# Moving one filler block from in front of unit 5's A product to behind its y transposes, and unit 3's v cast one SiLU sooner

## Chip, cores and metric

One core of one Trainium2 chip. The time is device microseconds (us) of that core; lower is better. Each launch gives one time, and a profile can be taken with it.

## The reference

A linear-attention recurrence (batch 4, 8 heads, 768 tokens, head size 48) followed by a two-layer network with a SiLU (3072 tokens, width 384, hidden 2048):

```python
for t in range(S):
    cur = einsum('bhd,bhe->bhde', u * kt, vt)
    y[:, :, t] = einsum('bhd,bhde->bhe', rt, state + cur)
    state = w[None, :, :, None] * state + einsum('bhd,bhe->bhde', kt, vt)
x = y.transpose(0, 2, 1, 3).reshape(B * S, H * D)
h = x @ w_in                       # 384 -> 2048
out = (h / (1 + exp(-h))) @ w_out  # 2048 -> 384
```

## The kernel before

The sequence is cut into 6 chunks of 128 tokens; a "unit" is one chunk of one of the 4 batches, 24 in all. A unit's chain runs over several engines: transposes of r and k on TensorE (PE; `tr`, `tk` or `xs`), decays on VectorE (DVE; `rk`), the A product on PE (`ae`, `ao`), its mask on DVE (`am`), the y product on PE, the addition of the bonus `vu` on DVE (`y16`), transposes of y on PE (`yT`) and their copy on ScalarE (ACT; `xT`). GpSimd (POOL) makes the bonus (`ku`, `rku_f`, `vu`), scaled keys (`kc`) and decayed states (`sdec`).

So that PE has work while a unit's chain runs elsewhere, the network is cut into "fillers" in a list: a hidden block of the first layer (three matmuls here, weight 0.5, ended by a SiLU on ACT), or a quarter of an output of the second layer (four matmuls, weight 1). `fill(n)` takes blocks of weight n off the front of the list. The trace before shows PE and ACT taking their instructions in the order in which they are written: unit 3's y product waits until 25.48 us and the filler written behind it starts only then, at 25.68; and ACT casts unit 3's v at 24.93, without a pause behind the two SiLUs that began at 24.32, though POOL's `vu` had begun to read the same input at 23.75. (Weight loads, a row of their own called PEld, ran ahead there: the first for that product came at 24.99.)

```python
    def p2(i, spins=0, nxt=None, late=False):      # A product, then the masks
        ...
        for p in range(NP):
            nc.tensor.matmul(ae[:, p, :], L["kT"][0:D, p, :], L["rT"][0:D, p, :], ...)
            nc.tensor.matmul(ao[:, p, :], L["kT"][64:PR, p, :], L["rT"][64:PR, p, :], ...)
        if nxt is not None:
            p1t(nxt)                               # the next unit's transposes, xs
        for a in (ae, ao):
            nc.vector.tensor_tensor(out=am, in0=a, in1=maskM..., op=ALU.mult)

    def l1(sc, ft, b0=0, b1=B):                    # a hidden block
        hps = ps.tile([128, B * C], FP, name="hps", tag="moe", bufs=3)
        ...
        nc.scalar.activation(out=gts[sc][:, ft, b0 * C:b1 * C], in_=hps, func=AF.Silu)

    def fill(n):
        owed[0] = min(owed[0] + n, n + 1.0)
        while fillers and owed[0] > 0.01:
            w_, f = fillers.pop(0)
            owed[0] -= w_
            f()

    # unit 3                                  # unit 5 (b_)
    p2(3)                                     fill(.5)
    nc.scalar.copy(out=st[3], in_=zero)       p2(b_, nxt=b_ + 1, late=True)
    fill(1)                                   fill(1.5)
    nat_v(3)    # v cast on ACT               p3y(b_)     # y product
    fill(1)                                   p3e(b_)     # y16 on DVE
    p3y(3)                                    ...
    p3e(3)                                    fill(.5)
    ...                                       p4(b_)      # yT on PE, xT on ACT
                                              fill(1)
```

(The last block sets two places of the program side by side.)

## Time and profile before

| | before |
|---|---|
| median of 4 runs | 202.06 us (201.87 to 202.56) |
| span of the profiled run | 200.4 us |
| PE busy | 192.2 us, 96% |
| granted TensorE clock, profiled run | 0.997 of full |
| PE idle between 24 and 66 us | 1.66 us |
| PE idle between 66 and 194.7 us | none |

A row of the timeline below gives start, length, engine, line of the kernel, operation, tiles out and in, sizes and count; in brackets stands the idle time of the engine just before and what ended it. "hps" is a hidden block, "ops" an output quarter.

### The profile page before, as it was taken

What the parts mean: (1) busy time and instruction counts of PE and PEld (TensorE: products, weight loads), DVE (VectorE), ACT (ScalarE), POOL (GpSimd) and SP (SyncE); (2) the same over time, 40 slices, a digit from 0 to 9 for tenths busy, and PEclk for the clock granted to TensorE, in tenths of its full rate; (3) what the DMA queues carried; (4) which work ended last, traced back from release to release, by engine and by line L of the source; (5) the groups of instructions that cost most, each with busy time, mean ns of one, the idle gap of its engine ahead of it and who ended that gap; (6) DMA issues with size and microseconds to landing.
All of it is one profiled execution on the core that took longest, in us unless ns stands there. A gap on an engine that the chain in (4) does not pass through costs nothing.

```text
span 200.4 us, 5014 instructions
## 1 busy us (share of the span) xinstructions
PE 192.2 (96%) x1973; PEld 129.8 (65%) x1973; DVE 115.1 (57%) x233; ACT 98.1 (49%) x225; POOL 115.1 (57%) x145
## 2 busy tenths in 40 slices
PE   7889999899999999999999999999999999999993
PEld 2646878787766876765666764666764666644563
DVE  6787658885758539594646864646863635510121
ACT  2556587799132651139662039662039661069300
POOL 3499869989975674867593767481748370100000
PEclk9999999999999999999999999999999999999998
DMA  4999998999999922688721738201120001210022
GB/s 85 205 182 176 206 210 169 163 186 196 193 191 265 229 42 64 136 185 176 140 55 41 160 108 167 44 0 43 39 83 0 0 3 41 77 44 0 0 78 79
DMA packets 82207, 22.34 MB, mean 111 GB/s; under 512 B 75400, under 2 KB 82184, under 8 KB 82184
## 3 DMA queue, kind: packets, MB, share of 16 engines
q1 hardware_dynamic: 78504, 18.88, 43.7%
q0 software_dynamic: 3680, 3.15, 10.6%
q8 instruction: 15, 0.25, 0.5%
q14 instruction: 8, 0.07, 0.1%
HBM read 20.45 MB, written 4.72 MB: 126 GB/s over the span
## 4 chain that ended last, share of the span: by engine, by line
PE 86%; issue 4%; POOL 4%; DVE 3%; ACT 2%; POOLq 0%; DVEq 0%
PE ops L366 30%; PE hps L354 29%; PE ae L267 11%; PE xs L242 4%; PE y L293 3%; PE yT L342 2%; PE y L290 2%; PE sps L309 1%; PE ops L380 1%; DVE am L276 1%; POOL rku_f L186 1%; POOL ku L180 1%; DVE y L300 1%; ACT xT L343 1%; PE ao L269 1%
## 5 line engine op out<-in xcount | busy, mean ns | idle before, releaser
L357 ACT ACTIVATE gT<-hps 128x256 f16<-128x256 f32 (+1 forms) x128 | 59.6, 494 | 24.2 <-PE hps L354 22.4
L354 PE MATMUL hps<-xT,win 128*128 128x256 f16 (+1 forms) x384 | 69.9, 326 | 0.9 <-ACT xT L343 0.4
L366 PE MATMUL ops<-wout,gT 128*128 128x384 f16 x368 | 65.5, 326 | 0.0
L354 PEld LDWEIGHTS <-win 128*128 128x128 f16 x384 | 35.1, 98 | 22.7 <-issue 1.7
L366 PEld LDWEIGHTS <-gT 128*128 128x128 f16 x368 | 34.2, 98 | 21.1
L343 ACT COPY xT<-yT 128x384 f16<-128x384 f16 x24 | 11.4, 476 | 58.2 <-PE yT L342 58.1
L276 DVE TENSOR_TENSOR am<-ae,maskM 128x512 f16<-128x512 f32 x24 | 16.6, 692 | 36.6 <-PE ao L269 36.4
L203 POOL TENSOR_TENSOR vu<-vin,rku 128x384 f32<-128x384 f32 x23 | 19.1, 831 | 19.4 <-DVE rku L197 19.3
L370 DVE COPY osb<-ops 128x384 f32<-128x384 f32 x23 | 12.8, 556 | 29.2 <-PE ops L366 29.1
L267 PE MATMUL ae<-rk 48*128 48x128 f32 x192 | 27.7, 285 | 0.7 <-DVE rk L230 0.7
L267 PEld LDWEIGHTS ae<-rk 48*128 48x128 f32 x192 | 23.1, 187 | 7.9 <-issue 5.3
L269 PE MATMUL ao<-rk 48*128 48x128 f32 x192 | 27.7, 285 | 0.0
L253 DVE TENSOR_TENSOR rk<-xs,pif 112x512 f32<-112x512 f32 x40 | 25.6, 681 | 1.7 <-PE xs L242 1.7
L186 POOL TENSOR_TENSOR rku_f<-rin,ku 128x384 f32<-128x384 f32 x24 | 24.1, 1005 | 1.9
L180 POOL TENSOR_TENSOR ku<-kin,u_bc 128x384 f32<-128x384 f32 x24 | 24.1, 1005 | 1.6 <-DMA kin<-in_k_dram 1.5
L191 POOL TENSOR_TENSOR kc<-kin,lamC 128x384 f16<-128x384 f32 x24 | 24.1, 1005 | 0.0
L269 PEld LDWEIGHTS ao<-rk 48*128 48x128 f32 x192 | 23.1, 187 | 0.0
L323 POOL CAST stb<-st 112x384 f16<-112x384 f32 x12 | 6.0, 504 | 25.8 <-DVE st L318 25.8
L300 DVE TENSOR_TENSOR y<-y,vu 128x384 f16<-128x384 f32 x24 | 13.3, 554 | 8.6 <-PE y L293 7.2
L276 DVE TENSOR_TENSOR am<-ao,maskM 128x512 f16<-128x512 f32 x24 | 16.3, 681 | 0.0
L325 POOL TENSOR_TENSOR sdec<-st,pif 112x384 f32<-112x384 f32 x16 | 13.4, 838 | 2.2 <-ACT gT L357 1.1
L197 DVE TENSOR_REDUCE rku<-rku_f 128x8 f32<-128x384 f32 x24 | 13.2, 549 | 2.0 <-POOL rku_f L186 1.6
(74 smaller groups left out, 188.6 us busy)
## 6 DMA issues: line engine op xcount, KB each, us to landing
rin<-in_r_dram SPq DMA_DIRECT2D x24, 192.0 KB, 3.6
kin<-in_k_dram SPq DMA_DIRECT2D x24, 192.0 KB, 3.7
vin<-in_v_dram SPq DMA_DIRECT2D x24, 192.0 KB, 3.6
out_dram<-osb SPq DMA_DIRECT2D x23, 192.0 KB, 2.0
win<-in_moe_w_in_dram POOLq DMA_DIRECT2D x4, 384.0 KB, 5.8
wout<-in_moe_w_out_dram POOLq DMA_DIRECT2D x2, 768.0 KB, 10.5
out_dram<-osh SPq DMA_DIRECT2D x1, 128.0 KB, 1.7
out_dram<-osh SPq DMA_DIRECT2D x1, 64.0 KB, 1.5
```

Of the source, the lines that this page charges most:

```text
L180: nc.gpsimd.tensor_tensor(out=L["ku"], in0=kin[i % NIN][:, :, 0:D], in1=u_bc, op=ALU.mult)
L186: nc.gpsimd.tensor_tensor(out=L["rku_f"], in0=rin[i % NIN][:, :, 0:D], in1=L["ku"], op=ALU.mult)
L191: nc.gpsimd.tensor_tensor(out=kc[i % NKC][:, :, 0:D], in0=kin[n][:, :, 0:D], in1=lamC, op=ALU.mult)
L203: nc.gpsimd.tensor_tensor(out=L["vu"], in0=vin[i % NIN], in1=L["rku"].unsqueeze(2).broadcast_to([128, H, D]), op=ALU.mult)
L253: nc.vector.tensor_tensor(out=rk[:, :, :, 64 * g:64 * g + 64], in0=xs[g][0:PR], in1=lam(g), op=ALU.mult)
L267: nc.tensor.matmul(ae[:, p, :], L["kT"][0:D, p, :], L["rT"][0:D, p, :], start=True, stop=True)
L269: nc.tensor.matmul(ao[:, p, :], L["kT"][64:PR, p, :], L["rT"][64:PR, p, :], start=True, stop=True)
L276: nc.vector.tensor_tensor(out=am, in0=a, in1=maskM.unsqueeze(1).broadcast_to([128, NP, C]), op=ALU.mult)
L300: nc.vector.tensor_tensor(out=L["y16"], in0=L["y"], in1=L["vu"], op=ALU.add)
L354: nc.tensor.matmul(hps, win[:, q, ft * 128:(ft + 1) * 128], xts[sc][:, q, b0:b1, :].rearrange("p b t -> p (b t)"), start=(q == 0), stop=(q ...
L357: nc.scalar.activation(out=gts[sc][:, ft, b0 * C:b1 * C], in_=hps, func=AF.Silu)
L366: nc.tensor.matmul(ops, gts[sc][:, ft, b * C:(b + 1) * C], wout[:, ft, :], start=(ft == 0), stop=(ft == NFT - 1))
```

## The change

The aim is to take two waits from PE: the one of unit 3's y product for its v cast, and the one for the copy of unit 5's transposes, which blocks the first hidden block of the next chunk.

```diff
     p2(3)
+    fill(.5)
+    nat_v(3)
+    fill(1.5)
     nc.scalar.copy(out=st[3], in_=zero)
-    fill(1)
-    nat_v(3)
-    fill(1)
     p3y(3)
@@
         load(NIN + i)
-    fill(.5)
     p2(b_, nxt=b_ + 1, late=True)
     fill(1.5)
     p3y(b_)
```

Nothing is added to replace the `fill(.5)`: the list is simply one block behind from there on, so every later `fill` takes something else than before until the list runs empty near 87 us.

## The prediction

> **What bounds the kernel now.** I read the page first, its busy rows and its slices.
>
> ```profile
> span 200.4 us, 5014 instructions
> PE 192.2 (96%) x1973; PEld 129.8 (65%) x1973; DVE 115.1 (57%) x233; ACT 98.1 (49%) x225; POOL 115.1 (57%) x145
> ...
> PE   7889999899999999999999999999999999999993
> ...
> PEclk9999999999999999999999999999999999999998
> ```
>
> TensorE (PE) is busy for 96% of the span at full granted clock. The change adds and removes no instruction, so only PE's 8.2 us of idle time can change. A table of stretches (start:end, length, PE busy, ...) says where the idle time lies.
>
> ```profile
> 24.00:27.50 3.50, 3.22 (x37) 2.35 (x34) 1.72 (x3) 2.94 (x9) 1.89 (x3) 1.00 1.16 231
> 27.50:37.50 10.00, 9.91 (x152) 8.60 (x152) 8.21 (x17) 7.85 (x22) 9.05 (x11) 1.00 0.96 178
> 37.50:48.50 11.00, 10.10 (x134) 8.32 (x133) 8.17 (x18) 9.18 (x27) 9.76 (x12) 1.00 1.23 178
> 48.50:63.00 14.50, 14.50 (x162) 10.04 (x161) 9.62 (x19) 4.03 (x10) 10.77 (x12) 1.00 1.01 205
> 63.00:66.00 3.00, 2.61 (x25) 1.95 (x25) 1.40 (x3) 2.31 (x7) 2.56 (x4) 1.00 1.05 269
> 66.00:194.70 128.70, 128.70 (x1264) 82.36 (x1263) 67.85 (x127) 59.19 (x119) 63.06 (x74) 1.00 0.32 75
> ```
>
> Idle is 0.28, 0.09, 0.90, 0.00 and 0.39 us in the first five rows and nothing in the sixth; the remaining 6.5 us lie before 24 us and in the last result, which the change does not touch. So 1.66 us, 0.8% of the span, is all that can be won. The timeline names the waits (start, length, engine, line, what, and in brackets the idle time and its releaser):
>
> ```profile
> 24.32 0.71 ACT L357 ACTIVATE gT<-hps 128x256 f16<-128x256 f32 x2 [0.64 <-PE hps L354]
> 24.93 0.50 ACT L175 CAST v<-vin 128x384 f16<-128x384 f32 x1
> 25.48 0.36 PE L293 MATMUL y<-v,am 128*128 128x48 f16 x8 [0.22 <-ACT v L175]
> ...
> 39.03 0.34 PE L342 MATMUL yT<-ident,y 128*128 128x128 f16 x3 [0.22 <-DVE y L300]
> 39.41 0.48 ACT L343 COPY xT<-yT 128x384 f16<-128x384 f16 x1 [0.18 <-PE yT L342]
> 39.94 1.14 PE L354 MATMUL hps<-xT,win 128*128 128x256 f16 x9 [0.40 <-ACT xT L343]
> ...
> 47.21 0.56 DVE L300 TENSOR_TENSOR y<-y,vu 128x384 f16<-128x384 f32 x1 [1.24 <-POOL vu L203]
> 47.82 0.34 PE L342 MATMUL yT<-ident,y 128*128 128x128 f16 x3 [0.28 <-DVE y L300]
> ...
> 65.00 0.81 PE L354 MATMUL hps<-xT,win 128*128 128x256 f16 x6 [0.39 <-ACT gT L357]
> ```
>
> Four waits: unit 3's y product for its v cast; unit 5's transposes for y and then the first hidden block (three matmuls) of the second chunk for ACT's copy of those transposes; unit 6's transposes, held by a GpSimd (POOL) chain that ends in vu; and at 65 us a hidden block for a SiLU that must free its PSUM slot. Bracketed idle is short of the true loss, as a matmul's end is modelled late. From starts alone, at 0.11 us per 256-column matmul, the loss at 65.00 is 65.00-63.47-9x0.11=0.54 us.
>
> [...] y's first weights loaded at 24.99 us, its matmul and every filler behind it waited to 25.48. [...] the v cast had its data long before and ran at 24.93 behind two SiLUs. [...] six such matmuls take 0.66 us in the chain of work, 110 ns each. [...] the longest PE wait in this middle part is 0.40 us and the granted clock there is 1.00[...].
>
> **Part one, unit 3's cast.** In order on ACT, before: state-zero copy, two SiLUs, v cast, six SiLUs in pieces. After: one SiLU, v cast, three SiLUs, zero copy, two SiLUs, then the transposes' copy. Successive starts put a SiLU at 0.33 us and the cast at 0.40 us of ACT time. The cast then starts near 24.65 and ends near 25.15; the second masked A product ends at 24.49+0.68=25.17; PE has issued its four fillers by 23.78+12x0.11=25.10. So y starts at 25.20 in place of 25.48: **0.28 us won**, and v, A and PE are then all equally late. Part is given back: two of the four SiLUs are now later, and the hidden blocks have three PSUM slots. The fifth block needs the second SiLU, 24.65+0.40+0.38=25.43, so it starts near 25.48 where 25.38 would do (0.10 lost). The zero copy (0.43 us), formerly done in ACT's 0.64 us pause at 23.7-24.3, now stands before two SiLUs, so the last block starts some 0.05-0.1 late. Left by unit 4's transposes (27.49): **about 0.17 us**. What follows (DVE's rk, unit 4's A product at 30.32) is released by PE or DVE, so it moves along.
>
> **Part two, unit 5's block.** One block is 3x0.11=0.33 us. Unit 5's A product can start 0.33 us sooner: its PSUM slots are long free. But its mask on DVE cannot:
>
> ```profile
> 35.12 0.55 DVE L197 TENSOR_REDUCE rku<-rku_f 128x8 f32<-128x384 f32 x1
> 35.70 0.74 DVE L318 TENSOR_TENSOR st<-sps,sdec 48x192 f32<-48x192 f32 x2
> 36.47 0.69 DVE L276 TENSOR_TENSOR am<-ae,maskM 128x512 f16<-128x512 f32 x1
> 37.08 0.68 DVE L276 TENSOR_TENSOR am<-ao,maskM 128x512 f16<-128x512 f32 x1
> 38.41 0.56 DVE L300 TENSOR_TENSOR y<-y,vu 128x384 f16<-128x384 f32 x1 [0.65 <-PE y L293]
> ```
>
> DVE runs without a pause from unit 4's masks (31.51) to 37.76, where the second mask of unit 5 ends; PE then began y at 37.65. With the block gone PE gets there 0.33 us sooner and **waits for DVE instead**. So y(5), and all behind it, gain only part one's 0.17 to 0.2 us. Behind the transposes the block fills PE while ACT copies: the loss there (39.94 less 39.20+0.17, so 0.57) falls to about 0.24. But the first block of the new chunk still needs that copy and starts at 39.94-0.19=39.75. PE is then free sooner, having a block less to do before unit 6's A product, but the POOL chain (two sdec from 40.94, ku, rku_f, kc, sdec, vu to 47.18, without a pause that matters) was started by DVE's st, which follows y(5). It too moves by 0.19, so unit 6's transposes start at 47.63, with one block (0.33 us) not yet done: its wait grows from 0.28 to some 0.6. Balance there: -0.19+0.33 = **+0.14 us**; alone, parts one and two would lose a little.
>
> **Part three, what the shift does later.** The filler list stays one block behind. I followed its order in the two built programs: from unit 6's transposes on, a hidden block changes place with an output quarter (four matmuls, 4x0.1625=0.65 us) until the list runs empty near 87 us, after which the order is the same to the end. The one place that matters is 65 us. Before: transposes, then five hidden blocks, of which the fourth needs the first's SiLU, and ACT stands at the transposes' copy (0.48) and the rT cast (0.62) until 64.56. After: transposes, one output quarter, then four hidden blocks. The quarter covers ACT's copy and cast: the first SiLU can run when its block ends, and the fourth block finds its slot. **0.54 us won.** Elsewhere from 48.5 to 63 us PE has no idle now, and DVE, ACT and POOL have slack, so the new order should open no new wait.
>
> Sum: +0.14-0.54 = -0.40 us. 202.09-0.40 = 201.69; call it 201.7.
>
> **The rivals.** (1) The naive account: each filled wait is won in full, 0.28+0.33+0.54 = 1.15 us, giving 200.9. Against it stand the gapless DVE row and the POOL chain, neither of which the change shortens. (2) The POOL chain takes all and the 65 us wait is only halved, say because the first SiLU still queues behind the copy and the cast: +0.14-0.2, giving 202.0, no difference to be seen. For it: ACT's order at that place is nearly unchanged. (3) A new wait: the zero copy now among the SiLUs, or the hidden blocks' three slots, costs more than the cast wins, giving 202.3. For it: ACT has only 0.2 us of pauses left between 24.3 and 28. Against: the fifth to eighth block each need a SiLU done about 0.05 us before, by the sums above.
>
> **Range and chances.** The three rivals span 200.9 to 202.3, all within 0.6% of before, and the three runs of before spread by 0.7 us themselves. I take 201.7, and 201.2 to 202.2 for 8 in 10. No path reaches 4 us either way: PE's remaining idle after 24 us is under 2 us, and nothing is added. Same 0.98, faster 0.01, slower 0.01.
>
> **What would show each step.** Part one is right if y(3) starts near 25.2 with no wait for v and unit 4's transposes near 27.3. Part two is right if y(5)'s matmuls now show a wait of about 0.3 us for DVE's am, the wait for xT falls to about 0.24, and unit 6's transposes wait about 0.6 us for y. If those transposes start before 47.4, the DVE and POOL bound is wrong and the gain is larger. Part three is right if no wait for a SiLU is left at 65 us and PE's busy time stays at 192.2 while the span falls by about 0.4. A wait over 0.2 us that is not in the list would prove the sum wrong, as would any change after 87 us.

The sum stands as +0.14-0.54=-0.40 us, from 202.09 to 201.69. Its times per matmul can be read in the chain of work of the kernel before: six matmuls of hidden blocks (256 columns) take 0.66 us (at 26.90), so 0.11 each, and twelve of output quarters (384 columns) 1.95 us (at 48.49), so 0.1625 each. That a matmul's end is modelled late is seen at y(3): by its length it ends at 25.48+0.36=25.84 us, but the filler behind it starts at 25.68. What is cut about the clock was not shown by any run; measured is a granted clock of 1.00 in every row of the table above and of the one in the result.

## The result

| | before | after |
|---|---|---|
| median | 202.06 us | 201.79 us |
| range, runs | 201.87 to 202.56, 4 | 201.41 to 201.95, 4 |
| span of the profiled run | 200.4 us | 200.2 us |

The ratio is 0.998 (95% interval 0.9957 to 1.0003). A ratio is the mean time of one kernel's fast runs over the mean of the other's in the same rounds, so it isn't quite the ratio of the medians. By this alone the change can't be told from nothing; a repetition with more rounds, below, gave 0.9963 (0.9946 to 0.998).

Effects this small are read in the traces. What differs from run to run is mostly the start (the first of unit 3's filler blocks began between 23.55 and 24.48 us in these traces), so I measure a **stretch**: from that block, the first of four, which stands in front of every difference, to the start of the last output product (as `--critical` gives it, that is, when the product before it has ended; the timeline's start is 0.16 us earlier in every trace). It is 194.69-23.78=170.91 us before and 194.41-23.84=170.57 us after, 0.34 us less. It repeats well: the second trace of the changed kernel gave 170.57 again. The kernel before was traced only once, so all differences from 170.91 rest on that one trace.

The page after, first lines, and then the same table of stretches as in the prediction (start:end, length, PE busy, ...):

```profile
span 200.2 us, 5013 instructions
...
PE 192.0 (96%) x1973; PEld 129.8 (65%) x1973; DVE 115.1 (58%) x233; ACT 97.9 (49%) x225; POOL 115.2 (58%) x145
```

```profile
24.00:27.50 3.50, 3.46 (x41) 2.63 (x41) 1.79 (x3) 3.12 (x11) 2.08 (x3) 1.00 1.19 232
27.50:37.50 10.00, 9.76 (x151) 8.42 (x147) 8.42 (x17) 7.99 (x23) 9.77 (x12) 1.00 0.94 183
37.50:48.50 11.00, 10.07 (x131) 8.40 (x132) 7.97 (x18) 8.81 (x26) 9.75 (x12) 1.00 1.26 183
48.50:63.00 14.50, 14.50 (x164) 10.11 (x163) 9.91 (x19) 4.18 (x10) 10.66 (x13) 1.00 0.92 187
63.00:66.00 3.00, 3.00 (x32) 2.25 (x31) 1.11 (x2) 2.40 (x6) 2.21 (x4) 1.00 1.09 264
```

Idle went from 0.28 to 0.04 us in the first row and from 0.39 to 0 in the last. But in the second it grew from 0.09 to 0.24, and in the third, where the change wanted to fill a wait, it is 0.93 us where it was 0.90. The timeline says why:

```profile
24.66 0.50 ACT L175 CAST v<-vin 128x384 f16<-128x384 f32 x1
25.22 0.42 PE L293 MATMUL y<-v,am 128*128 128x48 f16 x8
...
37.62 0.20 PE L293 MATMUL y<-v,am 128*128 128x48 f16 x1 [0.27 <-DVE am L276]
...
38.83 0.34 PE L342 MATMUL yT<-ident,y 128*128 128x128 f16 x3 [0.22 <-DVE y L300]
39.21 0.48 ACT L343 COPY xT<-yT 128x384 f16<-128x384 f16 x1 [0.18 <-PE yT L342]
39.74 0.49 PE L354 MATMUL hps<-xT,win 128*128 128x256 f16 x3
...
46.99 0.56 DVE L300 TENSOR_TENSOR y<-y,vu 128x384 f16<-128x384 f32 x1 [1.55 <-POOL vu L203]
47.61 0.34 PE L342 MATMUL yT<-ident,y 128*128 128x128 f16 x3 [0.52 <-DVE y L300]
```

Unit 3's wait is gone. Unit 5's wait for the copy is short now (39.74 has no bracket). In its place y(5) waits 0.27 us for its mask, at 37.62, and the wait in front of unit 6's transposes has grown from 0.28 to 0.52 us. So at unit 6 the changed kernel is 0.27 us ahead, by part one, but owes one block of 0.33 us: nothing is gained yet on balance. What part two wins is won at the fourth place, near 65 us:

```profile
62.76 0.33 PE L342 MATMUL yT<-ident,y 128*128 128x128 f16 x3
62.93 0.81 PE L366 MATMUL ops<-wout,gT 128*128 128x384 f16 x4
63.58 1.63 PE L354 MATMUL hps<-xT,win 128*128 128x256 f16 x12
63.78 0.56 DVE L370 COPY osb<-ops 128x384 f32<-128x384 f32 x1 [1.03 <-PE ops L366]
...
64.39 0.53 PEld L354 LDWEIGHTS <-win 128*128 128x128 f16 x5 [0.17 <-issue]
```

An output quarter (ops) now stands between unit 8's transposes and the hidden blocks, and covers ACT's copy and cast there. The weight loads (PEld) pause once, at 64.39, until the output copy on DVE has ended (63.78+0.56=64.34).

The balance, each time counted from unit 3's first filler block (23.78 before, 23.84 after):

| place | before | after | difference |
|---|---|---|---|
| y(3) starts | 1.70 | 1.38 | -0.32 |
| unit 4's input transposes, near 27.4 us | 3.71 | 3.45 | -0.26 |
| unit 6's y transposes | 24.04 | 23.77 | -0.27 |
| unit 9's A product, behind the place at 65 us | 41.97 | 41.30 | -0.67 |
| last output product | 170.91 | 170.57 | -0.34 |

At unit 9's A product the changed kernel still has one block, 0.33 us, to do that the other has done; 0.67-0.33=0.34, which is the end result. So all is settled by 66 us.

(The second line of the table is what the prediction's part one calls unit 4's transposes: the `xs` transposes of r and k that follow unit 3.)

The page alone doesn't show this: span and PE's busy time both fell by 0.2 us, so PE's idle time is 8.2 us as before. What it lost between 24 and 66 us (1.21 us in place of 1.66) is made up by more idle before 24 us, where the two programs are alike (3.79 us in place of 3.46).

### The profile page after: what moved, and what is told of

Its sections match the earlier page's. It is cut to its first block, busy times and chain, and to the rows that moved or that the text cites. A ratio compares the mean times of both kernels' runs of the same rounds, so it can differ in the third digit from the quotient of the medians.

```text
span 200.2 us, 5013 instructions
## 1 busy us (share of the span) xinstructions
PE 192.0 (96%) x1973; PEld 129.8 (65%) x1973; DVE 115.1 (58%) x233; ACT 97.9 (49%) x225; POOL 115.2 (58%) x145
## 4 chain that ended last, share of the span: by engine, by line
PE 84%; DVE 6%; POOL 4%; issue 3%; ACT 1%; DVEq 0%; POOLq 0%
PE ops L366 30%; PE hps L354 28%; PE ae L267 10%; PE xs L242 4%; PE y L293 3%; PE yT L342 2%; DVE am L276 2%; PE y L290 2%; POOL ku L180 1%; PE ops L380 1%; PE sps L309 1%; PE spin L125 1%; DVE pif L156 1%; POOL rku_f L186 1%; DVE y L300 1%
```

## The experiments

**Theory.** Part one moves everything by what y(3) gains. Part two wins nothing at units 5 and 6, because DVE's masks set y(5) and a POOL chain sets unit 6's transposes; it even leaves a block undone. Its one gain is a side effect downstream: the order at 65 us. **Rival.** Each wait is PE's alone and a block put into it is won. All times and stretches are in one table at the end of this section. All kernels gave correct results.

### Each part alone

`a1_cast_only` is the kernel before with the first hunk of the diff, `a2_block_only` with the second.

> Before with unit 3's part alone (v cast one SiLU sooner, zero copy behind the SiLUs). My theory: y(3) starts 0.3 us sooner, about 0.26 us is left at unit 4's transposes and moves down unchanged: unit 6's transposes 0.26 us earlier against the start of unit 3's fillers, the wait for a SiLU at 65 us stays at 0.39, the stretch from unit 3's fillers to the last product 170.65 us (170.91 before, 170.57 after). Rival (all four waits are won one by one, none is a bound of another engine): the same here; this run fixes the size of part one.

> Before with unit 5's part alone (the half filler taken out in front of its A product). My theory: DVE's masks and the GpSimd chain hold unit 5 and 6, so y(5) waits about 0.3 us for DVE and unit 6's transposes start when they did (24.04 us after unit 3's fillers, within 0.05), with one block still to do; the gain comes at 65 us alone, the output quarter covering ACT's copy: 0.54 there less 0.14 for a wait for the output copy on DVE, less 0.33 for the block: stretch from unit 3's fillers to the last product about 170.85 us, nearly nothing. Rival (the block fills the wait for the copy and is won in full): unit 6's transposes start about 0.33 us sooner, the stretch is 170.2.

The cast alone gave a stretch of 194.35-23.73=170.62 us, so -0.29. The block alone gave 194.83-24.01=170.82 us, so -0.09, with unit 6's transposes at 48.05-24.01=24.04 us, to the hundredth where they were, though PE had one block less to do before them. The rival wanted -0.33 there. From the trace of the block alone:

```profile
38.06 0.20 PE L293 MATMUL y<-v,am 128*128 128x48 f16 x1 [0.27 <-DVE am L276]
...
48.05 0.34 PE L342 MATMUL yT<-ident,y 128*128 128x128 f16 x3 [0.52 <-DVE y L300]
```

Both new waits are there without part one: they belong to the block. The two parts add to -0.38 where the change has -0.34, so most of the change is the cast.

> The changed kernel again with five rounds, for its interval: both theories 0.3 us under before (ratio 0.9985); stretch from unit 3's fillers to the last product 170.57 us as in its first trace.

`a3_after_again` is the changed kernel: 194.38-23.81=170.57 us, 201.78 us, ratio 0.9963. The ratio is further from 1 than in the first measurement because the kernel before ran at 202.56 us (median) in these rounds; I trust the stretch more for sizes.

### The block given back in front of unit 6

```diff
     sums(3)
     state(3)
-    fill(1)
+    fill(1.5)
```

on the changed kernel brings the list into step again before unit 6's A product.

> The changed kernel with the missing block given back in front of unit 6's A product (a filler of 1.5 in place of 1 there), so that the list is in step from then on and the order at 65 us is as before. My theory: unit 6's transposes start as in after (23.77 us after unit 3's fillers) since the GpSimd chain sets them, their wait shrinks from 0.52 to about 0.2-0.28, and the wait for a SiLU at 65 us (0.39) is back: stretch to the last product 170.91-0.27=170.64 us. So the block costs nothing put in front of unit 6. Rival (PE is what is late at unit 6): transposes 0.33 us later than in after, the wait at 65 us back, stretch 170.9 or more.

```profile
47.62 0.34 PE L342 MATMUL yT<-ident,y 128*128 128x128 f16 x3 [0.31 <-DVE y L300]
...
64.79 0.81 PE L354 MATMUL hps<-xT,win 128*128 128x256 f16 x6 [0.39 <-ACT gT L357]
```

Unit 6's transposes start at 47.62-23.86=23.76 us, as in the changed kernel, although PE did 0.33 us more work before them; the wait shrank to 0.31. And with the old order back, the wait of 0.39 us near 65 us is back too. Stretch 194.48-23.86=170.62, the same as the cast alone. So the whole worth of part two beyond part one is the order at 65 us: 0.40 us there, less the block of 0.33 us that was left undone. What remains is small: 0.05 us in this comparison (170.62-170.57), 0.09 us by `a2_block_only`.

### The POOL chain shortened

On the changed kernel, one operation (`sdec` of unit 3's state, 0.84 us) is moved behind unit 6's `vu`; nothing needs it before unit 7's state.

```diff
-    state(3)
+    state(3, dec=False)        # without its sdec
     fill(1)
...
         bonus_sum(i)
         bonus_vu(i)
+        if i == B + 2:
+            decay(3)           # the sdec left out above
```

> The changed kernel with one GpSimd operation (unit 3's decay, sdec, 0.84 us) moved behind unit 6's vu; nothing needs it before unit 7's state. My theory: the GpSimd chain sets unit 6's transposes in the changed kernel, so vu(6) ends some 0.65 us sooner, the wait of 0.52 us there is gone (PE gets there at about 23.1 us after unit 3's fillers, 23.77 in after), and the stretch to the last product is 170.57-0.64=169.93 us. Rival (another engine, PE or ACT, is what is late there): transposes where they were, stretch 170.5.

```profile
46.26 0.56 DVE L300 TENSOR_TENSOR y<-y,vu 128x384 f16<-128x384 f32 x1 [0.94 <-POOL vu L203]
...
46.87 0.34 PE L345 MATMUL yT<-ident,y 128*128 128x128 f16 x3
```

The transposes start at 46.87-23.71=23.16 us (23.77 in the changed kernel) and PE no longer waits. Stretch 193.66-23.71=169.95 us, 0.62 less than the changed kernel; time 201.11 us, ratio 0.9945. No PE, DVE or ACT work was touched, so POOL's chain is shown to be what held unit 6.

### DVE relieved by ACT

On the changed kernel, unit 1's two state copies (0.71 us, in DVE's gapless row in front of unit 5's masks) go to ACT.

```diff
-                nc.vector.tensor_copy(out=dst, in_=sps[...])
+                cp = nc.scalar.copy if i == 1 else nc.vector.tensor_copy
+                cp(out=dst, in_=sps[...])
```

> The changed kernel with unit 1's two state copies out of PSUM (0.71 us on DVE, between unit 4's y and unit 5's masks) done by ACT, which has pauses there. My theory: DVE's gapless row sets y(5), so the masks end 0.7 us sooner, y(5)'s wait for DVE (0.27) is gone, y(5) ends about 0.45 us sooner and the GpSimd chain and unit 6's transposes move by as much: 23.3 us after unit 3's fillers (23.77 in after), stretch to the last product 170.1 us. Rival (ACT is as full as DVE there, so the wait only changes its owner): y(5) waits for rT or v from ACT, and nothing is won, 170.5 or more.

Half came. The second mask ended at 36.30+0.68-23.76=13.22 us, against 36.88+0.68-23.84=13.72 in the changed kernel, 0.50 sooner, and y(5) has no wait for it. But PE itself came later, because of unit 6's input transposes:

```profile
35.50 0.65 PE L242 MATMUL xs<-ident,rin 64*112 64x64 f32 x8
...
36.30 1.16 PE L355 MATMUL hps<-xT,win 128*128 128x256 f16 x9
```

The sixteen transposes took from 35.50 to 36.30, 0.80 us; in the changed kernel they take from 35.58 to 36.13, 0.55 us. In the built program the second of their two PSUM tiles now got another slot: the one of unit 4's `sps`, which DVE frees only with unit 4's state addition, ended at 34.86+0.73=35.59. (In the changed kernel it got that of unit 4's `yT`, freed earlier by ACT's copy.) So the wait changed its owner, neither to the rT nor to the v of the rival's wording, but to a buffer. Stretch 194.10-23.76=170.34 us, -0.23 where -0.45 was expected. DVE's row is confirmed as y(5)'s bound; how much it costs is not separated from the slot.

### The shift alone, put where PE never waits

On the kernel before, without any part of the change:

```diff
-        fill(2)
+        fill(1.5 if i == B + 3 else 2)   # in front of unit 7's y
```

> The kernel before, with half a filler left out in front of unit 7's y, where PE never waits; unit 3 and unit 5 as before. The list is then behind by as much as in the changed kernel, and the order at 65 us is the same. My theory: unit 6's transposes as before (24.04), and 0.40 us won at 65 us (0.54 less 0.14 for the output copy on DVE that the third block waits for): stretch 170.91-0.40=170.51 us. So this one edit, with no part of the change in it, is worth as much as the whole change. Rival (the gain comes from filling the wait for unit 5's copy): nothing won, 170.9.

```profile
62.99 0.81 PE L366 MATMUL ops<-wout,gT 128*128 128x384 f16 x4
63.65 1.63 PE L354 MATMUL hps<-xT,win 128*128 128x256 f16 x12
```

The order is that of the changed kernel, and the bracketed wait for a SiLU is gone. Stretch 194.46-23.97=170.49 us, so -0.42: one edit that fills none of the waits the change aimed at, and in its one trace it wins more than the change. The times don't show it: median 202.27, ratio 1.0001 (0.9979 to 1.0022), with runs from 201.36 to 203.02. A gain of 0.42 of 202.2 us would be a ratio of 0.9979, the very end of the interval, so only the trace speaks for it.

### The order on ACT at 65 us

On the kernel before, PE untouched: ACT's rT cast for unit 9 is issued behind the SiLUs.

```diff
-        if i + 1 < NU:
+        if i + 1 < NU and i != B + 4:
             r16(i + 1)
...
         fill(2)
+        if i == B + 4:
+            r16(i + 1)
```

> The kernel before with one ACT operation moved: the rT cast for unit 9 (0.62 us), which stands in front of the SiLUs at 65 us, is issued behind five of them. PE's order is not changed. My theory: the wait at 65 us is ACT's queue order, copy and cast ahead of the first SiLU; without the cast the SiLU runs as the first block ends, the wait of 0.39 us is gone, 0.5 us won by starts: stretch from unit 3's fillers to the last product 170.91-0.50=170.41 us, more than the whole change wins. Rival (the output copy on DVE or the copy of the transposes alone holds that place): at most 0.2 us won, 170.7.

Its profile fell in a run (223.61 us, at a mean granted clock of 0.855); the other five took 201.75 to 202.05 us, at 0.997 to 1.0. So a slow state exists for this one-core program; what the chip's other cores did then isn't recorded. It was run again:

> The same kernel as before it (unit 9's rT cast behind five SiLUs, nothing else), again because its profile fell in the slow state (granted clock 0.855), so that no stretch could be read. Its times, 201.99 us and ratio 0.9976, agree with my theory of 0.5 us. In a trace of the fast state: the wait for a SiLU at 65 us (0.39) is gone and the stretch from unit 3's fillers to the last product is 170.41 us; by the rival, 170.7.

This trace was disturbed at its start: PE waited 0.64 us for weights of the first layer just before the stretch begins, and inside it 0.19 us more for these and 0.63 us for those of the second, so its stretch, 195.77-24.48=171.29 us, can't be compared. (An estimate: it is 0.11 us behind at unit 6, 48.63-24.48=24.15 for 24.04, and by starts the last wait is 51.23-49.14-8x0.1625=0.79; without both it would be 170.39, where 170.41 was expected.) The place itself can be compared:

```profile
65.06 1.83 PE L354 MATMUL hps<-xT,win 128*128 128x256 f16 x15
...
65.64 1.68 ACT L357 ACTIVATE gT<-hps 128x256 f16<-128x256 f32 x5
67.21 0.61 ACT L259 CAST rT<-rk 112x512 f16<-112x512 f32 x1
```

Five hidden blocks run as one row without a wait. From unit 8's transposes to unit 9's A product it takes 66.83-64.90=1.93 us, before 65.75-63.30=2.45: 0.52 us less. From there to the last product both kernels take 128.94 us. The times agree in direction (ratio 0.9976, 0.9962 to 0.999, then 0.9954, 0.9905 to 1.0004). So the wait at 65 us was the order on ACT: copy, cast, then the SiLU that frees a slot; the 0.62 us cast in front of that SiLU cost PE 0.52 us. The rival of this run (the copy alone, or DVE) is out.

### Two candidates

`c2_step_late_decay` takes the changed kernel, the late `sdec`, the block given back in front of unit 6 and the shift in front of unit 7.

> A candidate to beat both: the changed kernel, its missing block given back in front of unit 6's A product, half a filler left out in front of unit 7's y, and unit 3's decay behind unit 6's vu. Theory: 0.29 us of part one, 0.35 at unit 6's transposes (PE is then just in time) and 0.40 at 65 us: stretch 170.91-1.04=169.87 us, about 1.0 us under before (ratio 0.995). Rival (gains at unit 6 are given back later, to the weights of the second layer that land near 48 us): 170.3.

Stretch 194.03-23.55=170.48 us, 201.59 us: worse than the late `sdec` alone. At unit 6 its sum nearly held: the transposes start at 47.02-23.55=23.47 us, 0.57 sooner than before, for 0.29+0.35=0.64 told. What failed is the rest, as the rival had it: PE got to the third output quarter before the second half of the weights had come:

```profile
49.37 0.32 PE L369 MATMUL ops<-wout,gT 128*128 128x384 f16 x1 [0.38 <-DMA wout<-in_moe_w_out_dram]
```

By starts that wait is 49.37-47.52-8x0.1625=0.55 us, which is nearly the whole miss (170.48 for 169.87). Being one block behind there, as the changed kernel is, has this one real use.

`f1_all` takes the changed kernel, the late `sdec`, unit 1's state copies on ACT, `fill(2.5 if i == B + 3 else 2)` in front of unit 7's y and unit 9's rT cast behind the SiLUs.

> A candidate to beat both and the late-decay kernel: the changed kernel with unit 3's decay behind unit 6's vu, unit 1's state copies on ACT, the missing block made good in front of unit 7's y (after the second half of the second layer's weights has landed), and unit 9's rT cast behind the SiLUs. Theory: 169.95 us of the late-decay kernel, less 0.22 for the copies on ACT, less 0.1 for the place at 65 us (0.5 there in place of 0.4): stretch 169.6 us, ratio to before 0.993. Rival (a wait for the weights, as in the step-late-decay kernel, or ACT's fuller queue): 170.1 or more.

> The late-decay kernel again beside the last candidate on the same chip: stretch 169.95 us as in its first trace, ratio 0.9945. If the candidate's theory holds it is 0.3 us slower than the candidate, if the rival holds it is the faster of the two.

Stretch 193.75-24.11=169.64 us for `f1_all` (169.6 expected) and 193.94-23.98=169.96 for the late `sdec` again. Their medians in the same rounds are 201.04 and 201.13, so by time alone they are equal, and both beat the kernel before: ratios 0.9928 (0.9912 to 0.9943) and 0.9939 (0.9926 to 0.9952). The changed kernel wasn't in these rounds; by stretch they beat it too.

### All runs

| run | median us | ratio to before (95%) | stretch us | against 170.91 |
|---|---|---|---|---|
| the change | 201.79 | 0.998 (0.9957 to 1.0003) | 170.57 | -0.34 |
| a1_cast_only | 201.97 | 0.9972 (0.9954 to 0.999) | 170.62 | -0.29 |
| a2_block_only | 202.15 | 0.9981 (0.9964 to 0.9997) | 170.82 | -0.09 |
| a3_after_again | 201.78 | 0.9963 (0.9946 to 0.998) | 170.57 | -0.34 |
| a4_back_in_step | 202.20 | 0.9982 (0.9965 to 0.9999) | 170.62 | -0.29 |
| b1_decay_late | 201.11 | 0.9945 (0.9932 to 0.9957) | 169.95 | -0.96 |
| b2_state_on_act | 201.54 | 0.9967 (0.9955 to 0.9978) | 170.34 | -0.57 |
| b3_shift_late | 202.27 | 1.0001 (0.9979 to 1.0022) | 170.49 | -0.42 |
| c2_step_late_decay | 201.59 | 0.997 (0.9954 to 0.9986) | 170.48 | -0.43 |
| e1_cast_after_silu | 201.99 | 0.9976 (0.9962 to 0.999) | slow | |
| e2_cast_after_silu | 201.91 | 0.9954 (0.9905 to 1.0004) | disturbed | |
| f1_all | 201.04 | 0.9928 (0.9912 to 0.9943) | 169.64 | -1.27 |
| b1_again | 201.13 | 0.9939 (0.9926 to 0.9952) | 169.96 | -0.95 |

## Why the prediction was right

**Bound and ceiling.** Right: PE's busy time is unchanged within 0.2 us, and behind 88 us nothing differs but the offset. The time, 201.79 us, lies 0.1 us from the 201.7 given; as the runs of one kernel spread by about half a microsecond, that nearness is partly luck. So is the sum: -0.40 us told and -0.34 measured on the stretch, with part one some 0.1 us too low and part three 0.14 us too high, two errors that partly cancel. One sign, a span that falls by about 0.4 us at unchanged busy time, isn't seen on the page (0.2, and 0.2 less busy).

**Part one.** The mechanism held and its size was low: y(3) came 0.32 us sooner for 0.28 told, and 0.26 was left at the next transposes for 0.17. Of the two losses put against it, the fifth block's is there (0.08: it starts 0.28 us behind y, before 0.20); the one from the zero copy between the SiLUs isn't: from the seventh block to the transposes it takes 0.75 us in both kernels.

**Part two.** Right, and nearest to the mark: y(5) waits for DVE (0.27 shown, about 0.3 told), the wait for the copy fell to 39.74-39.34-0.17=0.23 (0.24 told), unit 6's transposes started at 47.61 (47.63 told). Their wait is 0.52 by the bracket, for "some 0.6", which was reckoned from a bracket; by starts it is 47.61-45.62-12x0.11=0.67, against 47.82-46.07-12x0.11=0.43 before, so it grew by 0.24 where a whole block, 0.33, was told. The runs `a2_block_only`, `a4_back_in_step` and `b1_decay_late` show the bound, `b2_state_on_act` the half of it that lies on DVE. Only the balance there, +0.14, was really +0.06, by part one's better gain.

**Part three.** The mechanism was right, as `e2_cast_after_silu` and `b3_shift_late` show, and the size too high: 0.40 us for 0.54 (0.06 to -0.34 in the balance). The term left out is a new wait of 64.39-63.58-6x0.11=0.15 us: the third hidden block takes the PSUM slot of the output that the quarter has just ended, and must wait for DVE to copy it (63.78 to 64.34). The prediction looked only at the SiLU's slots. Before, the transposes lay between the output's end and the blocks and hid that copy: it ended at 63.50+0.56=64.06, and the third block began, by starts, at 63.47+6x0.11=64.13.

**The rivals.** The naive account, 200.9 us, was wrong by a factor of three in the gain. The second (the place at 65 us only half won, -0.06 in all) was too low, but a part of that place was indeed not won, for another reason than the one it named. The third, a wait from the zero copy, did not come.

**What isn't settled.** Why executions begin by up to 0.9 us differently (unit 3's fillers start between 23.55 and 24.48 us in these traces, of programs that are alike up to there) was not studied; in the latest of them, `e2_cast_after_silu`, 0.64 us of it is a wait for weights. Nor was how much the landing of transfers varies: there PE waited 0.64 and 0.63 us for weights, for which the kernel before, with the same loads, shows no wait. The sizes above rest on one trace each, but for the two kernels traced twice, the changed one and the late `sdec`.

## What to carry to other kernels

Filling a wait with work won nothing here where another engine held what came next: `a2_block_only` took a block of 0.33 us from in front of unit 6's transposes and left them at 24.04 us. So follow the chain of the engine named in the bracket to its start, for here POOL and DVE merely handed the slack on to the next unit (its wait went from 0.28 to 0.52 us). In a list of fillers like this one, removing one shifts all that come after: read the new order to where the lists meet again, since the gain or the loss may lie far downstream (here at 65 us, 25 us behind unit 5's transposes). And ask of each shared pool who frees each slot: two of the larger errors here (part three, 0.15 us, and the copies on ACT, -0.23 where -0.45 was expected) had to do with a buffer freed by another engine than the one looked at.
